# Causal convolution and RWKV channel mix on one core: a convolution in 64x64 tiles of TensorE, and three scalings per step on GpSimd

## Chip, cores and metric

The kernel runs on one core of a Trainium2 chip. The metric is device time of the launch in microseconds (us); lower is better.

## What is computed

The input x is [8, 4160, 192]. A light-weight convolution comes first: each of 8 heads owns 24 channels and has 7 taps, softmax-normalised, and an output row is the weighted sum of its own row and the six before it. The result y goes into an RWKV channel mix with d_ff = 1024:

```
y[b,s,h,:]  = sum_k softmax(weight[h])[k] * x_pad[b, s+k, h, :]      (6 zero rows ahead)
y_prev      = y one row earlier (zero at the start)
xk          = mu_k*y + (1-mu_k)*y_prev
xr          = mu_r*y + (1-mu_r)*y_prev
k           = relu(xk @ w_k)
v           = (k*k) @ w_v
out         = sigmoid(xr @ w_r) * v
```

The kernel works in bf16 with fp32 accumulation and writes fp32.

## The kernel before

**Pairs and steps.** The eight batches form four pairs. Both batches of a pair (`s` in the code's tiles) are worked on together: their channels stand side by side, 64 of the one in partitions 0-63 and 64 of the other in 64-127, three thirds (`NC`) of 64 channels each. A pair is cut into steps of 512 rows (256 at both ends of the first pair; the 64 rows left over of all four pairs make one last step), 34 steps in all, numbered 0 to 33.

**Bundles.** The order of all instructions is written out by hand. The unit is the bundle: four slots of the K product (`k_mm`, L458: 64-row tiles of TensorE, one for each batch of the pair), then the R product (`r`, L532) of an earlier step, then a V product (`v`, L515: 32 matmuls of 128x128 weights and 192 columns), then one or two calls of the convolution (`conv`). A step of 512 rows has two bundles. Tables (`early`, `first`, `rq`, `xt`, `mixes`, `vq`, `vo`, `late`) say what runs in which bundle, and the loop at L701 to L722 walks through them: `early`, K and its relus on ScalarE (L487), R, V, `mixes`, three squares of k on VectorE (L501), `vo` (the product with r, L556, and the DMA of the output), `xt` (the convolution), the fourth square, `late`.

**Mixtures.** `diff` (L411) forms y - y_prev for a step in the bundle ahead of it, on VectorE; there, too, `mix(s, 0)` forms xk: three scalings by mu (L434, one for each third) and an add (L438). `mix(s, 1)` forms xr in the same way one bundle later (for steps of two bundles). All of it is VectorE's. xk and xr have two buffers, the differences three.

**PSUM.** One ring of four slots of two banks serves K, R, V and the convolution in the order of issue: per bundle four K slots, one R, one V and one for each call of the convolution. A slot comes free when its reader (relu, sigmoid, the product at L556, or the copies of the convolution) has ended.

**Convolution.** It runs in blocks of 120 output rows: 128 input rows (6 of halo, 2 unused) lie in partitions, and a banded 128x128 matrix per head, `toe`, is the stationary operand. Blocks are gathered in groups; the first pair has groups of 3, 4, 4 and 5 blocks, whose results go back to channel-major form by TensorE transposes (`tr`), and then of 10 and 9; the others have 10, 10, 10 and 5. The later groups ("large": `on_pe` is False, index g above 3) take the way through DRAM: ScalarE copies the result to `y` (`conv_out`, L324), SP writes it to `y_dram` (`y_write`, L337), and a transposing DMA reads it back to `yT` (`y_read`, L345). For a group of 10 blocks a head is one matmul of 480 columns (10 blocks x 2 batches x 24 channels, L285), which fills a bank; a call does two heads, with one ring slot. A head that crosses a boundary of 64 channels has two copies.

**Loads of x.** `x_tile` takes one of three `xb` buffers and clears what has to be zero; `load_x` issues the DMAs, which cast to bf16, on GpSimd's queue (POOL): one for each batch (L125), and a smaller one at the start (L119) and at the end (L124) of a sequence. `keep_tail` (L395) copies a pair's last rows on GpSimd. Nothing else runs on GpSimd in the steady state.

Of the kernel before, what the change touches and what calls it, by code (L numbers as in the profile page):

```python
# [7 lines left out]
FP32 = mybir.dt.float32  # L8
BF16 = mybir.dt.bfloat16
# [5 lines left out]
def kernel(  # L15
# [11 lines left out]
    nc = tc.nc  # L27
# [8 lines left out]
    NC = D // Q  # L36
    HALO = K - 1
    BLK = 120
    GB = 10
    NBLK = -(-S // BLK)  # L40
    BANK = 512
# [40 lines left out]
    last_bundle = [bundle_of[st[3] + st[4] - 1] for st in steps]  # L82


    groups = []
    for p in range(NPAIR):
        blk0 = 0
        for nb, s, on_pe in (
            ((3, 0, True), (4, 1, True), (4, 2, True), (5, 3, True), (10, 4, False), (9, 6, False))
            if p == 0  # L90
            else ((10, 0, False), (10, 2, False), (10, 4, False), (5, 7, False))
        ):
            groups.append((p, blk0, nb, first_bundle[first_step[p] + s], on_pe))
            blk0 += nb


# [2 lines left out]
    def x_tile(g):  # L99
        p, blk0, nb, _, _ = groups[g]  # L100
        xb = three.tile([P, GB, 2, D], BF16, tag="xb", name="xb")
        xbs[g] = xb
        if g > 4:

            nc.vector.memset(xb[0:1, 0, 0, 0:2], 0.0)  # L105
        if blk0 == 0:
            nc.gpsimd.memset(xb[0:32, 0, :, :], 0.0)
        if blk0 + nb == NBLK:
            nc.gpsimd.memset(xb[:, nb - 1, :, :], 0.0)

    def load_x(g):
        p, blk0, nb, _, _ = groups[g]
        xb = xbs[g]
        for s in range(2):
            b = 2 * p + s
            lo, hi = 0, nb
            if blk0 == 0:
                lo = 1
                nc.gpsimd.dma_start(out=xb[HALO:P, 0, s, :], in_=x[b, 0 : P - HALO, :])  # L119
            t0 = blk0 * BLK - HALO  # L120
            if blk0 + nb == NBLK:
                hi = nb - 1
                r0 = t0 + hi * BLK
                nc.gpsimd.dma_start(out=xb[0 : S - r0, hi, s, :], in_=x[b, r0:S, :])  # L124
            nc.gpsimd.dma_start(  # L125
                out=xb[:, lo:hi, s, :],
                in_=bass.AP(
                    tensor=x.tensor,
                    offset=x.offset + (b * S + t0 + lo * BLK) * D,
                    ap=[[D, P], [BLK * D, hi - lo], [1, D]],  # L130
                ),
            )
# [134 lines left out]
    ys, yTs, y_drams = {}, {}, {}  # L267
    conv_ps = {}

    def chunks(g):  # L270
        n = max(1, min(3, BANK // (2 * G * groups[g][2])))
        return [range(h, min(H, h + n)) for h in range(0, H, n)]


    def conv_mm(g, c):
        nb = groups[g][2]
        if c == 0:
            ys[g] = two.tile([P, GB, 2 * D], BF16, tag="y", name="y")
        ps2 = ring.tile([P, 2, BANK], FP32, tag="k", name="ps_c")
        for k, hs in enumerate(chunks(g)[c : c + 2]):  # L280
            w = G * len(hs)
            ps = ps2[:, k, 0 : nb * 2 * w].rearrange("p (n s c) -> p n s c", n=nb, s=2)
            conv_ps[g, c + k] = ps
            for i, h in enumerate(hs):
                nc.tensor.matmul(  # L285
                    out=ps[:, :, :, i * G : (i + 1) * G],
                    lhsT=toe[:, h, :],
                    rhs=xbs[g][:, :nb, :, h * G : (h + 1) * G],
                    start=True,
                    stop=True,  # L290
                )

    def conv_small(g, copies):

        nb = groups[g][2]
        ys[g] = [two.tile([P, 4, P], BF16, tag=f"y_small{i}", name="y_small") for i in range(NC)]
        tiles = [ring.tile([P, 2, BANK], FP32, tag="k", name="ps_c") for _ in range(3 if g == 0 else 2)]
        banks = [t[:, i, 0 : nb * P] for t, i in ((tiles[0], 0), (tiles[1], 0), (tiles[-1], 0 if g == 0 else 1))]
        for i, o in enumerate(banks):
            o = o.rearrange("p (n s c) -> p n s c", n=nb, s=2)  # L300
            c0, c1 = i * Q, (i + 1) * Q
            for h in range(c0 // G, -(-c1 // G)):
                a, b = max(c0, h * G), min(c1, h * G + G)
                nc.tensor.matmul(
                    out=o[:, :, :, a - c0 : b - c0],
                    lhsT=toe[:, h, :],
                    rhs=xbs[g][:, :nb, :, a:b],
                    start=True,
                    stop=True,
                )  # L310
        for i, o in enumerate(banks):
            copies[i](out=ys[g][i][:BLK, :nb, :].rearrange("p n c -> p (n c)"), in_=o[:BLK, :])

    def conv_out(g, c, copy):
        nb = groups[g][2]
        hs = chunks(g)[c]
        ps = conv_ps.pop((g, c))
        y = ys[g][:BLK, :nb, :].rearrange("p n (c s q) -> p n c s q", c=NC, s=2)
        c0, c1 = hs[0] * G, hs[-1] * G + G
        a = c0  # L320
        while a < c1:
            i = a // Q
            b = min(c1, (i + 1) * Q)
            copy(out=y[:, :, i, :, a - i * Q : b - i * Q], in_=ps[:BLK, :, :, a - c0 : b - c0])  # L324
            a = b

    def new_yT(p):
        yTs[p] = two.tile([P, 3, -(-(YC + NBLK * BLK) // 16) * 16], BF16, tag="yT", name="yT")
        y_drams[p] = dram.tile([NBLK * BLK, 2 * D], BF16, tag=f"y{p % 2}", name="y_dram")
        nc.vector.memset(yTs[p][:, :, 0:YC], 0.0)  # L330


    def y_write(g):
        p, blk0, nb, _, _ = groups[g]
        if blk0 == 0:
            new_yT(p)
        nc.sync.dma_start(  # L337
            out=y_drams[p][blk0 * BLK : (blk0 + nb) * BLK, :].rearrange("(n t) c -> t n c", t=BLK),
            in_=ys[g][:BLK, :nb, :],
        )  # L340

    def y_read(g):
        p, blk0, nb, _, _ = groups[g]
        r0, r1 = blk0 * BLK, min((blk0 + nb) * BLK, S)
        nc.sync.dma_start_transpose(  # L345
            out=yTs[p][:, :, YC + r0 : YC + r1], in_=y_drams[p][r0:r1, :]
        )
# [67 lines left out]
    def mix(s, i, sl=slice(0, NC)):  # L415

        L = steps[s][2]
        d = diffs[s]
        if sl.start == 0:
            (xks, xrs)[i][s] = two.tile([P, NC, STEP], BF16, tag=("xk", "xr")[i], name=("xk", "xr")[i])  # L420
        t = (xks, xrs)[i][s]
        if s == 0 and i == 0:
            c = sl.start
            nc.vector.scalar_tensor_tensor(
                out=t[:, c, :L],
                in0=d[:, c, :L],
                scalar=mu[:, i, c : c + 1],
                in1=y_of(s, sl, 0)[:, 0, :],
                op0=ALU.mult,
                op1=ALU.add,  # L430
            )
            return
        for c in range(sl.start, sl.stop):
            nc.vector.tensor_scalar(  # L434
                out=t[:, c, :L], in0=d[:, c, :L], scalar1=mu[:, i, c : c + 1], scalar2=None, op0=ALU.mult
            )
        o = shaped(s, t[:, sl, :L])
        nc.vector.tensor_tensor(out=o, in0=o, in1=y_of(s, sl, 0), op=ALU.add)  # L438
# [151 lines left out]
    def at(table, b, fn, *a):  # L590
        table.setdefault(b, []).append((fn, a))

    def conv(g, c):
        if g < 3:
            act_, dve_ = nc.scalar.copy, nc.vector.tensor_copy
            return conv_small(g, (act_, act_, dve_ if g == 0 else act_))
        conv_mm(g, c)
        for k in range(c, min(c + 2, len(chunks(g)))):
            conv_out(g, k, nc.scalar.copy)

    for g, (p, blk0, nb, fb, on_pe) in enumerate(groups):
        nx = 1 if g < 3 else -(-len(chunks(g)) // 2)
        if g == 0:
            continue
        if g == 1:
            xs = []
        elif p == 0:
            xs = {2: [0], 3: [1, 1], 4: [2, 2, 3, 3], 5: [4, 4, 5, 5]}[g]
        else:
            xs = range(fb - 10, fb - 10 + nx)  # L610
        for i, b in enumerate(xs):
            at(xt, b, conv, g, 2 * i)
        if on_pe:
            for j in range((nb + 3) // 4):
                at(first, g - 1, tr, g, j)
        else:
            at(late, xs[-1], y_write, g)

            at(late, xs[-1] + (1 if g == 4 else 2), y_read, g)
        if g > 3:  # L620

            b = {4: 1, 5: 1, 6: 2, 7: 8, 8: 10, 9: 13}.get(g)
            b = first_bundle[first_step[p]] + (-17, -13, -7, -4)[(g - 6) % 4] if b is None else b
            at(early, b, x_tile, g)
            at(early, b, load_x, g)
# [127 lines left out]
```

## Time and profile before

| | us |
|---|---|
| median of 13 runs | 436.01 (435.67 to 438.3) |
| profiled execution, whole | 436.23 |
| its span on the core | 434.4 |
| TensorE busy | 422.0 |
| VectorE busy | 380.1 |
| ScalarE busy | 349.1 |
| GpSimd busy | 48.6 |

One execution is profiled; its span is the time between the first and the last instruction on the core, and 1.8 us of the execution lie around it. L-numbers are lines of the kernel before. A timeline line gives the start, the duration from the first start to the last end, the engine, the line and the operation, the operands with their shapes, and how many instructions the line stands for; in brackets, how long the engine had been idle and what ended that. PE is TensorE, PEld its weight loads, DVE VectorE, ACT ScalarE, POOL GpSimd, SP SyncE. The ends of matmuls are modelled and overlap the next start, so lengths of stages on TensorE are taken from start to start. A line of the shares by stage holds the stretch, its length, the busy times (with the number of instructions) of PE, PEld, DVE, ACT and POOL, the granted clock of TensorE, the share of the DMA engines and GB/s.

### The profile page before, as it was taken

How to read it: one execution, taken by the hardware profiler on the slowest of the kernel's cores; microseconds unless marked ns; L12 is line 12 of the kernel's file. 1: busy time of each engine (PE TensorE's matmuls, PEld its weight loads, DVE VectorE, ACT ScalarE, POOL GpSimd, SP SyncE). 2: the span in 40 equal slices, each digit the busy share in tenths (PEclk: the TensorE clock that was granted, in tenths of full speed). 3: DMA queues.
4: the chain of work that ended last, by engine and by line, in shares of the span. 5: the costliest groups of instructions: out<-in, count | busy, mean ns of one | idle time of the engine just before them, and what ended most of it. 6: DMA issues, size and time to landing. Idle time of an engine off the chain costs nothing.

```text
span 434.4 us, 11361 instructions
## 1 busy us (share of the span) xinstructions
PE 422.0 (97%) x4709; PEld 294.7 (68%) x4709; DVE 380.1 (87%) x678; ACT 349.1 (80%) x474; POOL 48.6 (11%) x73
## 2 busy tenths in 40 slices
PE   8789999999999999999999999999999999999995
PEld 3465757766866776676677667766766776667785
DVE  6879879998988989889888998898898898999983
ACT  5788987988888788889888788988898788777780
POOL 7450001202300100202110100102000000000000
PEclk9999999999999999999999999999999999999999
DMA  8998666999797953879697982696744463421223
GB/s 133 192 154 141 177 172 130 210 199 178 174 175 206 176 163 93 129 184 184 172 177 164 186 171 79 136 229 127 179 118 129 123 159 117 114 66 47 74 74 110
DMA packets 134484, 64.30 MB, mean 148 GB/s; under 512 B 85132, under 2 KB 134048, under 8 KB 134432
## 3 DMA queue, kind: packets, MB, share of 16 engines
q1 hardware_dynamic: 96050, 48.31, 44.2%
q0 software_dynamic: 37488, 14.66, 29.1%
q8 instruction: 37, 0.61, 0.6%
q10 hardware_dynamic: 894, 0.61, 0.5%
q14 instruction: 15, 0.12, 0.1%
HBM read 29.92 MB, written 36.99 MB: 154 GB/s over the span
## 4 chain that ended last, share of the span: by engine, by line
PE 87%; DMA 5%; DVE 4%; ACT 1%; issue 1%; POOL 1%; SPq 0%; ACTq 0%
PE ps_v L515 39%; PE ps_k L458 36%; PE ps_r L532 7%; PE ps_c L285 4%; DMA wk<-in_moe_w_k_dram 2%; DMA y_dram<-y 2%; DMA yT<-y_dram 2%; DVE k L501 2%; ACT k_sb L487 1%; ACT y L324 1%; DVE yT L367 0%; DVE d L411 0%; DVE xk L434 0%; POOL xb L125 0%; PE ps_t L358 0%
## 5 line engine op out<-in xcount | busy, mean ns | idle before, releaser
L487 ACT ACTIVATE k_sb<-ps_k 128x1024 bf16<-128x1024 f32 x260 | 246.6, 1053 | 25.8 <-PE ps_k L458 25.3
L515 PE MATMUL ps_v<-wv,k 128*128 128x192 bf16 x2080 | 182.7, 246 | 1.3 <-ACT k_sb L487 1.3
L458 PE MATMUL ps_k<-xk,wk 64*128 64x512 bf16 (+1 forms) x1632 | 181.1, 367 | 2.4 <-DVE xk L438 1.0
L515 PEld LDWEIGHTS <-k 128*128 128x128 bf16 x2080 | 168.7, 98 | 11.3 <-issue 11.3
L501 DVE TENSOR_TENSOR k<-k_sb 128x1024 bf16<-128x1024 bf16 x260 | 167.8, 686 | 0.4 <-ACT k_sb L487 0.4
L458 PEld LDWEIGHTS <-wk 64*128 64x128 bf16 x1632 | 74.7, 94 | 97.6 <-issue 19.1
L556 DVE TENSOR_TENSOR o_sb<-ps_v,r_sb 128x768 f32<-128x768 f32 x64 | 61.2, 956 | 35.2 <-PE ps_v L515 33.3
L324 ACT CAST y<-ps_c 120x480 bf16<-120x480 f32 (+4 forms) x134 | 54.3, 483 | 44.1 <-PE ps_c L285 44.1
L540 ACT ACTIVATE r_sb<-ps_r 128x768 bf16<-128x768 f32 x65 | 56.4, 867 | 1.3 <-PE ps_r L532 1.3
L125 POOL DMA_DIRECT2D xb<-in_x_dram x34 | 30.8, 911 | 210.9 <-PE ps_k L458 165.0
L532 PEld LDWEIGHTS <-xr 64*128 64x128 bf16 x780 | 34.1, 94 | 16.8 <-issue 1.4
L532 PE MATMUL ps_r<-wr,xr 64*128 64x192 bf16 x780 | 42.9, 243 | 1.6 <-DVE xb L105 0.8
L434 DVE TENSOR_SCALAR xk<-d,mu 128x512 bf16<-128x512 bf16 (+1 forms) x99 | 33.0, 388 | 1.2
L411 DVE TENSOR_TENSOR d<-yT 128x1536 bf16<-128x1536 bf16 (+2 forms) x35 | 31.0, 887 | 1.9 <-DMA yT<-y_dram 1.8
L438 DVE TENSOR_TENSOR xr<-xr,yT 128x1536 bf16<-128x1536 bf16 (+1 forms) x33 | 31.0, 939 | 1.1
L438 DVE TENSOR_TENSOR xk<-xk,yT 128x1536 bf16<-128x1536 bf16 (+1 forms) x32 | 30.4, 950 | 1.1
L434 DVE TENSOR_SCALAR xr<-d,mu 128x512 bf16<-128x512 bf16 (+1 forms) x102 | 29.0, 339 | 0.0
L285 PE MATMUL ps_c<-xb,toe 128*128 128x480 bf16 (+2 forms) x120 | 28.7, 338 | 0.0
L285 PEld LDWEIGHTS <-toe 128*128 128x128 bf16 x120 | 11.0, 98 | 1.0
L395 POOL COPY y_tail<-yT 128x195 bf16<-128x195 bf16 x4 | 1.9, 484 | 78.4 <-DMA yT<-y_dram 78.4
L651 PE MATMUL warm<-zeros,ones_t 128*128 128x512 bf16 x16 | 6.3, 578 | 1.8 <-DVE zeros L666 1.8
L367 DVE COPY yT<-ps_t 128x720 bf16<-128x720 bf16 (+1 forms) x7 | 3.2, 500 | 4.1 <-PE ps_t L358 4.1
(52 smaller groups left out, 51.2 us busy)
## 6 DMA issues: line engine op xcount, KB each, us to landing
out_dram<-o_sb SPq DMA_DIRECT2D x128, 192.0 KB, 2.4
y_dram<-y SPq DMA_DIRECT2D x10, 900.0 KB, 6.4
xb<-in_x_dram POOLq DMA_DIRECT2D x14, 480.0 KB, 8.7
xb<-in_x_dram POOLq DMA_DIRECT2D x6, 432.0 KB, 6.4
xb<-in_x_dram POOLq DMA_DIRECT2D x10, 192.0 KB, 6.3
y_dram<-y SPq DMA_DIRECT2D x3, 450.0 KB, 3.9
y_dram<-y SPq DMA_DIRECT2D x1, 810.0 KB, 5.7
xb<-in_x_dram POOLq DMA_DIRECT2D x2, 384.0 KB, 7.3
```

Of the source, the lines that this page charges most:

```text
L285: nc.tensor.matmul(out=ps[:, :, :, i * G : (i + 1) * G], lhsT=toe[:, h, :], rhs=xbs[g][:, :nb, :, h * G : (h + 1) * G], start=True, stop=True,
L324: copy(out=y[:, :, i, :, a - i * Q : b - i * Q], in_=ps[:BLK, :, :, a - c0 : b - c0])
L411: nc.vector.tensor_tensor(out=shaped(s, diffs[s][:, cs, :L]), in0=y_of(s, cs, 1), in1=y_of(s, cs, 0), op=ALU.subtract)
L434: nc.vector.tensor_scalar(out=t[:, c, :L], in0=d[:, c, :L], scalar1=mu[:, i, c : c + 1], scalar2=None, op0=ALU.mult)
L438: nc.vector.tensor_tensor(out=o, in0=o, in1=y_of(s, sl, 0), op=ALU.add)
L458: nc.tensor.matmul(out=ps[:, i, f * L : (f + 1) * L], lhsT=wk[r, c, fs], rhs=xk[r, c, :L], start=c == 0 and f == 0, stop=c == NC - 1 and f ...
L487: nc.scalar.activation(out=k_sb, in_=ps.rearrange("p a b -> p (a b)"), func=AF.Relu)
L501: nc.vector.tensor_tensor(out=o, in0=i, in1=i, op=ALU.mult)
L515: nc.tensor.matmul(out=o, lhsT=k2s[s][:, f, t * P : (t + 1) * P], rhs=wv[:, f, :], start=(f == 0), stop=(f == NF - 1),)
L532: nc.tensor.matmul(out=ps[:, i, k * D : (k + 1) * D], lhsT=xr[q, c, ts], rhs=wr[q, c, :], start=c == 0, stop=c == NC - 1,)
L540: nc.scalar.activation(out=r_sbs[s, j], in_=ps[:, :, 0 : 2 * D], func=AF.Sigmoid)
L556: nc.vector.tensor_tensor(out=o_sb.rearrange("p (b t) d -> p b (t d)", b=2), in0=v_ps.pop((s, j)), in1=r_sbs.pop((s, j)), op=ALU.mult,)
```

## The change

For the large groups a block of 116 rows takes the place of one of 120. It holds two half blocks of 58 output rows. The first one's 64 input rows lie in partitions 0-63, the second one's in 64-127. Each head is then four matmuls with 64x64 weights (the two diagonal quarters of `toe`): input half i goes to bank i, and the first and the second half of the group's blocks (j) go to output partitions 0-63 and 64-127. For a group of 10 blocks a matmul has 240 columns, and a unit of two heads fills both banks of a slot; ScalarE copies both banks in one instruction (two where a boundary of 64 channels is crossed). The end groups have 10 blocks in the first pair and 6 in the others, and the latter stand one step earlier in the order. The loads have a DMA for each batch and half, and further ones for rows at either end of a sequence. The write to `y_dram` is four DMAs: for each half of the partitions, 48 rows and 10. The read begins and ends at multiples of 16 rows. The fourth group (g = 3) keeps 128x128 matmuls in a function of its own, with its copies after both banks' matmuls. From step 3 on, the three scalings of xr run on GpSimd; its add stays on VectorE.

```
-            ((3, 0, True), (4, 1, True), (4, 2, True), (5, 3, True), (10, 4, False), (9, 6, False))
+            ((3, 0, True), (4, 1, True), (4, 2, True), (5, 3, True), (10, 4, False), (10, 6, False))
             if p == 0
-            else ((10, 0, False), (10, 2, False), (10, 4, False), (5, 7, False))
+            else ((10, 0, False), (10, 2, False), (10, 4, False), (6, 6, False))
...
+    def load_x_halves(g):
+        p, _, nb, _, _ = groups[g]
+        xb = xbs[g]
+        for s in range(2):
+            b = 2 * p + s
+            for i in range(2):
+                full = []
+                for m in range(nb):
+                    r0 = base[g] + (2 * m + i) * HB - HALO
+                    lo, hi = max(0, -r0), min(Q, S - r0)
+                    if lo == 0 and hi == Q:
+                        full.append(m)
+                    elif hi > lo:
+                        nc.gpsimd.dma_start(
+                            out=xb[i * Q + lo : i * Q + hi, m, s, :], in_=x[b, r0 + lo : r0 + hi, :]
+                        )
+                nc.gpsimd.dma_start(
+                    out=xb[i * Q : (i + 1) * Q, full[0] : full[-1] + 1, s, :],
...
+    def conv_units(g):
+        n = min(H, BANK // (G * groups[g][2]))
         return [range(h, min(H, h + n)) for h in range(0, H, n)]
...
+        for k, h in enumerate(hs):
+            for j in range(2):
+                for i in range(2):
+                    nc.tensor.matmul(
+                        out=ps[j * Q : (j + 1) * Q, i, 0 : nb * w].rearrange("p (n s c) -> p n s c", n=nn, s=2)[
+                            :, :, :, k * G : (k + 1) * G
+                        ],
+                        lhsT=toe[i * Q : (i + 1) * Q, h, i * Q : (i + 1) * Q],
+                        rhs=xbs[g][i * Q : (i + 1) * Q, j * nn : (j + 1) * nn, :, h * G : (h + 1) * G],
+                        start=True,
+                        stop=True,
+                    )
...
     def conv_out(g, c, copy):
...
+        src = ps[:, :, 0 : nb * (c1 - c0)].rearrange("p i (n s c) -> p i n s c", n=nb // 2, s=2)
+        y = ys[g][:, :nb, :].rearrange("p (n i) (c s q) -> p i n c s q", i=2, c=NC, s=2)
+        for a, b in pieces(c0, c1):
+            copy(out=y[:, :, :, a // Q, :, a % Q : a % Q + b - a], in_=src[:, :, :, :, a - c0 : b - c0])
...
     def y_write(g):
...
+        for j in range(2):
+            r0 = base[g] + j * nb * HB
+            rows = y_drams[p][r0 : r0 + nb * HB, :].rearrange("(n t) c -> t n c", t=HB)
+            for t0, t1 in ((0, HB // 16 * 16), (HB // 16 * 16, HB)):
+                nc.sync.dma_start(out=rows[t0:t1], in_=ys[g][j * Q + t0 : j * Q + t1, :nb, :])
...
     def y_read(g):
...
-        r0, r1 = blk0 * BLK, min((blk0 + nb) * BLK, S)
+        r0 = base[g] // 16 * 16
+        r1 = min((base[g] + 2 * nb * HB) // 16 * 16, S)
...
+        eng = nc.gpsimd if i == 1 and s > 2 else nc.vector
         for c in range(sl.start, sl.stop):
-            nc.vector.tensor_scalar(
+            eng.tensor_scalar(
                 out=t[:, c, :L], in0=d[:, c, :L], scalar1=mu[:, i, c : c + 1], scalar2=None, op0=ALU.mult
             )
```

More of the change, by code (lines that the diff above doesn't have):

```diff
@@ L38 @@
     BLK = 120
+    HB = 58
     GB = 10
@@ L82 @@
     last_bundle = [bundle_of[st[3] + st[4] - 1] for st in steps]
-    groups = []
+    groups, base = [], []
     for p in range(NPAIR):
@@ L88 @@
         for nb, s, on_pe in (
-            ((3, 0, True), (4, 1, True), (4, 2, True), (5, 3, True), (10, 4, False), (9, 6, False))
+            ((3, 0, True), (4, 1, True), (4, 2, True), (5, 3, True), (10, 4, False), (10, 6, False))
             if p == 0
-            else ((10, 0, False), (10, 2, False), (10, 4, False), (5, 7, False))
+            else ((10, 0, False), (10, 2, False), (10, 4, False), (6, 6, False))
         ):
             groups.append((p, blk0, nb, first_bundle[first_step[p] + s], on_pe))
+            if on_pe:
+                base.append(blk0 * BLK)
+            elif groups[-2][4] or blk0 == 0:
+                base.append(blk0 * BLK)
+            else:
+                base.append(base[-1] + 2 * HB * groups[-2][2])
             blk0 += nb
@@ L107, in x_tile @@
             nc.gpsimd.memset(xb[0:32, 0, :, :], 0.0)
-        if blk0 + nb == NBLK:
+        if g > 3 and base[g] + 2 * HB * nb >= S:
             nc.gpsimd.memset(xb[:, nb - 1, :, :], 0.0)
+    def load_x_halves(g):
[16 more added lines that the diff above has]
+                    out=xb[i * Q : (i + 1) * Q, full[0] : full[-1] + 1, s, :],
+                    in_=bass.AP(
+                        tensor=x.tensor,
+                        offset=x.offset + (b * S + base[g] + (2 * full[0] + i) * HB - HALO) * D,
+                        ap=[[D, Q], [2 * HB * D, len(full)], [1, D]],
+                    ),
+                )
     def load_x(g):
         p, blk0, nb, _, _ = groups[g]
+        if g > 3:
+            return load_x_halves(g)
         xb = xbs[g]
@@ L120, in load_x @@
             t0 = blk0 * BLK - HALO
[L121 to L124, printed above, removed]
             nc.gpsimd.dma_start(
@@ L268, with pieces @@
     conv_ps = {}
-    def chunks(g):
-        n = max(1, min(3, BANK // (2 * G * groups[g][2])))
+    def pieces(c0, c1):
+        cuts = [c0] + [a for a in range(Q, D, Q) if c0 < a < c1] + [c1]
+        return list(zip(cuts, cuts[1:]))
+    def conv_units(g):
+        n = min(H, BANK // (G * groups[g][2]))
         return [range(h, min(H, h + n)) for h in range(0, H, n)]
@@ L278, in conv_mm, with conv_full @@
             ys[g] = two.tile([P, GB, 2 * D], BF16, tag="y", name="y")
-        ps2 = ring.tile([P, 2, BANK], FP32, tag="k", name="ps_c")
[L280 to L284, printed above, removed]
+        ps = ring.tile([P, 2, BANK], FP32, tag="k", name="ps_c")
+        hs = conv_units(g)[c]
+        w = G * len(hs)
+        nn = nb // 2
+        conv_ps[g, c] = ps
+        for k, h in enumerate(hs):
[9 more added lines that the diff above has]
+                        stop=True,
+                    )
+    def conv_full(g, c, copy):
+        nb = groups[g][2]
+        if c == 0:
+            ys[g] = two.tile([P, GB, 2 * D], BF16, tag="y", name="y")
+        y = ys[g][:BLK, :nb, :].rearrange("p n (c s q) -> p n c s q", c=NC, s=2)
+        ps2 = ring.tile([P, 2, BANK], FP32, tag="k", name="ps_c")
+        w = 2 * G
+        banks = [ps2[:, k, 0 : nb * 2 * w].rearrange("p (n s c) -> p n s c", n=nb, s=2) for k in range(2)]
+        for k, ps in enumerate(banks):
+            for i in range(2):
+                h = 4 * c + 2 * k + i
                 nc.tensor.matmul(
@@ L290, in conv_mm @@
                     stop=True,
+                )
+        for k, ps in enumerate(banks):
+            c0 = (4 * c + 2 * k) * G
+            for a, b in pieces(c0, c0 + w):
+                copy(
+                    out=y[:, :, a // Q, :, a % Q : a % Q + b - a], in_=ps[:BLK, :, :, a - c0 : b - c0]
                 )
@@ L315, in conv_out @@
         nb = groups[g][2]
-        hs = chunks(g)[c]
+        hs = conv_units(g)[c]
         ps = conv_ps.pop((g, c))
-        y = ys[g][:BLK, :nb, :].rearrange("p n (c s q) -> p n c s q", c=NC, s=2)
         c0, c1 = hs[0] * G, hs[-1] * G + G
[L320 to L325, printed above, removed]
+        src = ps[:, :, 0 : nb * (c1 - c0)].rearrange("p i (n s c) -> p i n s c", n=nb // 2, s=2)
+        y = ys[g][:, :nb, :].rearrange("p (n i) (c s q) -> p i n c s q", i=2, c=NC, s=2)
+        for a, b in pieces(c0, c1):
+            copy(out=y[:, :, :, a // Q, :, a % Q : a % Q + b - a], in_=src[:, :, :, :, a - c0 : b - c0])
     def new_yT(p):
         yTs[p] = two.tile([P, 3, -(-(YC + NBLK * BLK) // 16) * 16], BF16, tag="yT", name="yT")
-        y_drams[p] = dram.tile([NBLK * BLK, 2 * D], BF16, tag=f"y{p % 2}", name="y_dram")
+        y_drams[p] = dram.tile([S + 2 * P, 2 * D], BF16, tag=f"y{p % 2}", name="y_dram")
         nc.vector.memset(yTs[p][:, :, 0:YC], 0.0)
@@ L336, in y_write @@
             new_yT(p)
[L337 to L340, printed above, removed]
+        for j in range(2):
[3 more added lines that the diff above has]
+                nc.sync.dma_start(out=rows[t0:t1], in_=ys[g][j * Q + t0 : j * Q + t1, :nb, :])
     def y_read(g):
         p, blk0, nb, _, _ = groups[g]
-        r0, r1 = blk0 * BLK, min((blk0 + nb) * BLK, S)
+        r0 = base[g] // 16 * 16
+        r1 = min((base[g] + 2 * nb * HB) // 16 * 16, S)
         nc.sync.dma_start_transpose(
@@ L596, in conv @@
             return conv_small(g, (act_, act_, dve_ if g == 0 else act_))
+        if g == 3:
+            return conv_full(g, c, nc.scalar.copy)
         conv_mm(g, c)
-        for k in range(c, min(c + 2, len(chunks(g)))):
-            conv_out(g, k, nc.scalar.copy)
+        conv_out(g, c, nc.scalar.copy)
     for g, (p, blk0, nb, fb, on_pe) in enumerate(groups):
-        nx = 1 if g < 3 else -(-len(chunks(g)) // 2)
+        nx = len(conv_units(g))
         if g == 0:
@@ L611 @@
         for i, b in enumerate(xs):
-            at(xt, b, conv, g, 2 * i)
+            at(xt, b, conv, g, i)
         if on_pe:
```

## The prediction

> **What bounds the kernel.** The page's busy shares come first, then the shares by stage, then the timeline of one period.
>
> ```profile
> PE 422.0 (97%) x4709; PEld 294.7 (68%) x4709; DVE 380.1 (87%) x678; ACT 349.1 (80%) x474; POOL 48.6 (11%) x73
> ...
> 160.00:200.00 40.00, 40.00 (x449) 28.04 (x444) 35.85 (x63) 34.54 (x48) 5.28 (x8) 1.00 0.62 134
> ```
>
> From 80 us on TensorE never stops. Starts, not modelled ends, give the bundle's length: one with a convolution, then one without.
>
> ```profile
> 201.32 2.76 PE L458 MATMUL ps_k<-xk,wk 64*128 64x512 bf16 x24
> 203.92 0.66 PE L532 MATMUL ps_r<-wr,xr 64*128 64x192 bf16 x12
> 204.51 2.81 PE L515 MATMUL ps_v<-wv,k 128*128 128x192 bf16 x32
> 207.16 0.57 PE L285 MATMUL ps_c<-xb,toe 128*128 128x480 bf16 x2
> 207.66 2.77 PE L458 MATMUL ps_k<-xk,wk 64*128 64x512 bf16 x24
> ...
> 379.37 2.81 PE L515 MATMUL ps_v<-wv,k 128*128 128x192 bf16 x32
> 382.11 2.76 PE L458 MATMUL ps_k<-xk,wk 64*128 64x512 bf16 x24
> ```
>
> 6.34 us (207.66-201.32) against 5.94 (382.11 less 376.18, the K start before it). The convolution costs 0.50 before K, but V is followed after 2.65 instead of 2.74: 0.405 in all, 0.20 for 480 columns.
>
> VectorE is nearly full in every second bundle, that with `diff` (call it A):
>
> ```profile
> 202.50 0.95 DVE L411 TENSOR_TENSOR d<-yT 128x1536 bf16<-128x1536 bf16 x1
> 203.49 0.88 DVE L434 TENSOR_SCALAR xk<-d,mu 128x512 bf16<-128x512 bf16 x3
> 204.40 0.96 DVE L438 TENSOR_TENSOR xk<-xk,yT 128x1536 bf16<-128x1536 bf16 x1
> 205.28 1.89 DVE L501 TENSOR_TENSOR k<-k_sb 128x1024 bf16<-128x1024 bf16 x3
> 207.36 0.96 DVE L556 TENSOR_TENSOR o_sb<-ps_v,r_sb 128x768 f32<-128x768 f32 x1 [0.20 <-PE ps_v L515]
> ...
> 62.77 0.95 DVE L556 TENSOR_TENSOR o_sb<-ps_v,r_sb 128x768 f32<-128x768 f32 x1
> 63.77 1.47 PE L458 MATMUL ps_k<-xk,wk 64*128 64x512 bf16 x12 [0.22 <-DVE o_sb L556]
> ```
>
> It waits 0.20 us in A before `o_sb`, and 0.88 in the other bundle (B). The last two lines show what lateness hits: K's second half (its 13th matmul) needs the PSUM slot that `o_sb` frees. In the steady state that half is due at 207.66+1.30 = 208.96 and `o_sb` ends at 208.32, so A tolerates 0.20+0.64, about 0.8 us of VectorE delay.
>
> **What the Trainium skill says.** "TensorEngine Tiling (Array Packing)", Key Properties: a change of tiling mode drains TensorE. The trace agrees: V to K takes 2.74, V to the convolution in the same 128x128 mode 2.65, so 0.095 for a switch. "SBUF — State Buffer", Who interferes with whom: GpSimd's port pair is VectorE's second, held by one instruction at a time; it collides with two-port modes, and a VectorE operation with two SBUF inputs collides with a GpSimd one that reads SBUF. The trace shows both a cost and none:
>
> ```profile
> 103.50 0.83 DVE L501 TENSOR_TENSOR k<-k_sb 128x1024 bf16<-128x1024 bf16 x1
> 104.18 0.37 POOL L395 COPY y_tail<-yT 128x195 bf16<-128x195 bf16 x1
> 104.26 0.83 DVE L501 TENSOR_TENSOR k<-k_sb 128x1024 bf16<-128x1024 bf16 x1
> ...
> 377.75 0.95 DVE L411 TENSOR_TENSOR d<-yT 128x1536 bf16<-128x1536 bf16 x1
> 378.10 0.82 POOL L395 COPY y_tail<-yT 128x195 bf16<-128x195 bf16 x1 [78.36 <-DMA yT<-y_dram]
> 378.75 0.88 DVE L434 TENSOR_SCALAR xk<-d,mu 128x512 bf16<-128x512 bf16 x3
> ```
>
> Around the first copy two squares take 0.83 instead of 0.68, 0.30 together; so at the two copies near 199 and 299 us (three squares 2.19 instead of 1.89). At the fourth the copy waits, and VectorE loses nothing. "DMA: Bandwidth & Descriptors", how many engines: the outermost sizes decide it, 16 for 48 rows, 10 for 10; this trace doesn't show it.
>
> **The change, part by part.**
>
> *Convolution on TensorE.* Two matmuls of 480 become, per bundle, two heads of four 64x64 matmuls of 240. Bounds of a four: 0.10 if all run together (half of 0.20), 0.20 if only the row halves do. The closest spacing in the trace of a load and a matmul is R's, (0.59-0.095)/12 = 0.041, so four take 0.10 to 0.16 by that; I take 0.13. A bundle: 2x0.13, plus one more mode switch, 0.095, is 0.355: 0.05 saved on the path, in 11x4 = 44 bundles 2.2 us. The three end groups spend 2x0.405 each now; then three units (3, 3 and 2 heads), 8x0.13+3x0.095 = 1.33, so they lose 1.6. Sum: 0.6 us saved. Ends: 5 us saved (0.10: 44x0.11, end groups even), 10 if the switch costs nothing more, 6 lost (0.20: 44x0.095, plus 1.6).
>
> *ScalarE.* A group of ten has 6x0.570+2x0.447+2x0.311 = 4.9 us of copies (by-shape means). Two of 960 elements and two each of 640 and 320, at about 0.8 ns an element more, take 4.2. V waits for the second relu after these copies by little, so nothing is gained; at worst the single copy's later start costs V 0.1 in a bundle.
>
> *R's scalings.* 31 steps (3 to 33) move three instructions each, no DMA. VectorE loses 0.90 us of work in B, where it was idle for 0.88 already: no gain on the path. GpSimd starts them when `diff` ends, in A (xr's buffer has been read two bundles before). They follow x's memsets and DMA issues on POOL's queue, which wait for convolutions at least two bundles old; `y_tail`'s copy and later loads queue behind them, with 5 us or more to spare. GpSimd itself: its memset of 384 took 0.42 and of one element 0.10, 0.82 ns an element, so 512 with COPY's fixed 0.2 take about 0.62; three, 1.9, of the 5.4 us from `diff`'s end to R's add (203.45 to 208.84, where its scalings start now). With a six-issue load ahead the add may wait 1 us, a few times, inside B's idle time.
> What it takes from VectorE: COPY took 0.30 for 195 elements; 317 more at 0.82 ns give 0.56; a scaling of VectorE that it meets leaves the port idle for about 0.16 of its 0.29 pitch (0.345 against 0.279 for 256 elements, so 0.13 goes with the 512). I take 0.40 each; ends 0 (the copy at 378.10) and 0.79 (COPY's cost by elements). Three delay A by 1.2. Behind that stand xk's scalings, its add, the squares and `o_sb`. Late by 1.2, less the 0.80, and K's second half is due 0.05 earlier: a stall of 0.45. Without a convolution the fourth K tile is the one due, 382.11+1.95 = 384.06, against an `o_sb` that starts at 382.43: 0.68 to spare, stall 0.52. A bundles with a convolution: 23; without: 8. 23x0.45+8x0.52 = 14.5 us.
>
> *DRAM round trip.* Four issues on SP instead of one, about 0.4 us each (0.45 at most steady issues), ahead of out's writes; later reads come two bundles behind. Only the first large group is bare: its write (7.56 us) and read (7.35) are on the chain at 43 to 58 us, where VectorE waits 1.8 for them. I charge 0.5; ends -0.5 and 1.5.
>
> *x loads.* Four to six POOL issues for two to four, about 0.75 for half a transfer against 0.95; landing within 10 us, and the users come 30 us later. Nothing; without that cover a microsecond a group. The earlier slot of the end group and the fourth group's reordered copies: nothing.
>
> Sum: -0.6+14.5+0.5 = 14.4. The profiled execution took 436.23 (span 434.4, 1.8 around it), close to the median 436.01. I forecast **450 us**.
>
> **Rivals.** (1) *The port hardly matters*: GpSimd fits into VectorE's gaps, as at 378.10, and the fours run together. Decided by three scalings costing under 0.8 us: no stall, and 5 us saved, 431; with a free switch 426. For it: the clean slack in B, the fourth copy. Against: three of four copies cost. (2) *A wash*: the delay lies just at the 0.8 tolerance and a four takes 0.13-0.16: 435.5 to 437. (3) *The fours are serial*, 0.20, and the port costs 0.40: 6+14.5+0.5, 457; decided by weight loads that don't overlap. (4) *Full lock*, 0.56: A late by 1.7, stalls 0.9 to 1.0, 23x0.93+8x1.0 = 29: 465; at 0.79 beyond 480.
>
> **Numbers.** Forecast (437 to 455) 0.45; rival 1 0.27; rival 2 0.08; rival 3 0.10; rival 4 0.10. 0.2% is what a measurement of this kernel can tell from no change. Faster 0.28, same 0.07, slower 0.65. The range, 428 to 460, leaves out rival 4 and the best of rival 1. Both signs hold chance, but the likeliest case alone has 437 to 455.
>
> **What would show it.** Each step right: in A bundles VectorE's time from `diff` to `o_sb` grows by about 1.2 us and K's 13th matmul waits for `o_sb`; V-to-K with a convolution falls from 3.15 to 3.10. Wrong: TensorE's starts stay gapless and bundles are 6.24 or shorter (rival 1), or the convolution takes 0.5 and more (rival 3), or R's matmuls wait for GpSimd.

## Result and profile after

The changed kernel takes 467.81 us (median of 10 runs, 466.19 to 471.76) against 436.22 for the kernel before (46 runs): a ratio of 1.0728, interval 1.0712 to 1.0744. It is 31.6 us slower; the forecast was 450, with a range up to 460. The profiled execution's span is 466.4 us. From here on an L-number is a line of the kernel whose profile is shown.

First the page of the changed kernel: busy shares, TensorE's busy tenths and its granted clock in 40 slices. After them two stretches from the shares by stage, one with an end group's load and one without.

```profile
PE 429.8 (92%) x5045; PEld 301.1 (65%) x5045; DVE 374.1 (80%) x585; ACT 348.4 (75%) x427; POOL 232.0 (50%) x194
...
PE   7789999696999999996899999999599999999996
...
PEclk9999999999799999999799999999799999999999
```

```profile
200.00:240.00 40.00, 34.20 (x386) 23.92 (x384) 28.31 (x45) 26.90 (x33) 17.18 (x19) 0.91 0.64 139
...
360.00:400.00 40.00, 40.00 (x487) 28.14 (x482) 35.93 (x54) 33.12 (x40) 18.77 (x10) 1.00 0.57 142
```

VectorE is less busy than before (374 us in a longer span), so it has not become full. TensorE's row has three notches at nearly equal distances (the 6, 6 and 5 in slices 10, 19 and 29), each with a notch in the clock in the same slice or the next; an earlier one, in slice 8, has none. Between 360 and 400 us TensorE is busy throughout. So most of the loss is made in a few places. One of them, in order of time (`diff`, after which the scalings could start; VectorE's memset of one element; GpSimd's load issues and scalings; then what waits):

```profile
204.29 0.95 DVE L473 TENSOR_TENSOR d<-yT 128x1536 bf16<-128x1536 bf16 x1
...
210.37 0.06 DVE L112 MEMSET xb<- 1x1 uint32 x1
...
211.65 0.69 POOL L134 DMA_DIRECT2D xb<-in_x_dram  x1 [11.19 <-issue]
...
214.77 0.71 POOL L134 DMA_DIRECT2D xb<-in_x_dram  x1
...
215.51 4.65 POOL L497 TENSOR_SCALAR xr<-d,mu 128x512 bf16<-128x512 bf16 x3
...
220.19 1.08 DVE L501 TENSOR_TENSOR xr<-xr,yT 128x1536 bf16<-128x1536 bf16 x1 [9.76 <-POOL xr L497]
...
221.96 3.77 ACT L550 ACTIVATE k_sb<-ps_k 128x1024 bf16<-128x1024 f32 x4 [5.71 <-DVE k L564]
...
223.04 1.47 PE L521 MATMUL ps_k<-xk,wk 64*128 64x512 bf16 x6 [5.80 <-ACT k_sb L550]
...
225.40 4.18 PE L578 MATMUL ps_v<-wv,k 128*128 128x192 bf16 x32
```

GpSimd sat idle for 11.2 us: the end group's load stands ahead of the bundle's scalings on its queue, and did not start before VectorE had reached the memset that `x_tile` puts into the same bundle (1.2 us after it; the profile names no releaser here, but does in an experiment below). After six issues and three scalings R's add starts; VectorE has stood idle for 9.76 us. The squares stand behind the add in VectorE's order, the relus wait for the squares' buffers, and K waits for the relus' PSUM slots: 5.80 us without a matmul. Afterwards the clock is low (the trace has 0.50 granted between 222 and 228 us): V's 32 matmuls take 4.18 us instead of 2.81. From 223.04 to the next convolution at 229.50 there are 6.46 us for work that takes 4.0 at the usual spacing, so this place costs about 8.3. Waits of these three kinds in the changed kernel, added up (total, times, longest):

```profile
DVE xr L501 <- POOL xr L497: 45.3, 11, 9.8
...
PE ps_k L521 <- ACT k_sb L550: 16.9, 4, 5.8
...
PE ps_k L521 <- DVE o_sb L619: 5.6, 10, 1.7
```

The bundle that the prediction worked with, A, in the changed kernel. Compare `diff`, xk's scalings (0.88 before), the squares (1.89 before), `o_sb` and K:

```profile
347.37 0.95 DVE L473 TENSOR_TENSOR d<-yT 128x1536 bf16<-128x1536 bf16 x1
...
348.36 1.31 DVE L497 TENSOR_SCALAR xk<-d,mu 128x512 bf16<-128x512 bf16 x3
...
348.52 5.80 POOL L497 TENSOR_SCALAR xr<-d,mu 128x512 bf16<-128x512 bf16 x3 [6.86 <-DVE d L473]
...
350.59 2.30 DVE L564 TENSOR_TENSOR k<-k_sb 128x1024 bf16<-128x1024 bf16 x3
...
352.39 2.89 PE L521 MATMUL ps_k<-xk,wk 64*128 64x512 bf16 x24
352.51 1.02 ACT L385 CAST y<-ps_c 128x320 bf16<-128x320 f32 x2 [0.93 <-PE ps_c L321]
352.81 0.94 DVE L619 TENSOR_TENSOR o_sb<-ps_v,r_sb 128x768 f32<-128x768 f32 x1
```

VectorE loses 0.43 and 0.41, some 0.85 us in all, while three scalings run for 5.8 us beside it. The trace shows that just two of its instructions lose the time: the second of xk's scalings takes 0.78 us and its neighbours 0.35 and 0.34, and the second of the three squares takes 1.10 instead of 0.68. GpSimd loses too: its second scaling takes 2.50 us, the others 1.63 and 1.72. K is stretched by 0.13 only (2.89 for 2.76). The convolution, V to K:

```profile
245.56 2.81 PE L578 MATMUL ps_v<-wv,k 128*128 128x192 bf16 x32
...
248.30 0.40 PE L321 MATMUL ps_c<-xb,toe 64*64 64x240 bf16 x8
248.63 1.47 PE L521 MATMUL ps_k<-xk,wk 64*128 64x512 bf16 x12
```

3.07 us instead of 3.15.

### The profile page after: what moved, and what is told of

The parts are those of the page before. It is cut to its first block, busy times and chain, and to the rows that moved or that the text cites. A ratio compares the mean times of both kernels' runs of the same rounds, so it can differ in the third digit from the quotient of the medians.

```text
span 466.4 us, 12099 instructions
## 1 busy us (share of the span) xinstructions
PE 429.8 (92%) x5045; PEld 301.1 (65%) x5045; DVE 374.1 (80%) x585; ACT 348.4 (75%) x427; POOL 232.0 (50%) x194
## 5 line engine op out<-in xcount | busy, mean ns | idle before, releaser
L497 POOL TENSOR_SCALAR xr<-d,mu 128x512 bf16<-128x512 bf16 (+1 forms) x93 | 169.4, 1833 | 125.8 <-DVE d L473 84.2
L521 PE MATMUL ps_k<-xk,wk 64*128 64x512 bf16 (+1 forms) x1632 | 187.3, 370 | 25.7 <-ACT k_sb L550 16.9
L578 PE MATMUL ps_v<-wv,k 128*128 128x192 bf16 x2080 | 186.2, 249 | 1.3 <-ACT k_sb L550 1.3
L564 DVE TENSOR_TENSOR k<-k_sb 128x1024 bf16<-128x1024 bf16 x260 | 178.6, 726 | 1.6 <-ACT k_sb L550 1.4
L578 PEld LDWEIGHTS <-k 128*128 128x128 bf16 x2080 | 171.8, 99 | 12.1 <-issue 11.8
L385 ACT CAST y<-ps_c 128x960 bf16<-128x960 f32 (+7 forms) x81 | 50.7, 667 | 60.4 <-PE ps_c L321 60.4
L619 DVE TENSOR_TENSOR o_sb<-ps_v,r_sb 128x768 f32<-128x768 f32 x64 | 60.8, 950 | 26.8 <-PE ps_v L578 24.8
L134 POOL DMA_DIRECT2D xb<-in_x_dram x56 | 40.9, 737 | 72.6 <-issue 39.5
L497 DVE TENSOR_SCALAR xk<-d,mu 128x512 bf16<-128x512 bf16 (+1 forms) x99 | 39.6, 454 | 1.2
L321 PE MATMUL ps_c<-xb,toe 64*64 64x240 bf16 (+1 forms) x448 | 20.0, 265 | 0.0
L321 PEld LDWEIGHTS <-toe 64*64 64x64 bf16 x448 | 8.3, 105 | 7.7 <-issue 7.7
L131 POOL DMA_DIRECT2D xb<-in_x_dram x14 | 7.8, 556 | 2.9 <-DMA wr<-in_moe_w_r_dram 2.0
```

The lines of the kernel that those rows point to most:

```text
L134: nc.gpsimd.dma_start(out=xb[i * Q : (i + 1) * Q, full[0] : full[-1] + 1, s, :], in_=bass.AP(tensor=x.tensor, offset=x.offset + (b * S + b ...
L385: copy(out=y[:, :, :, a // Q, :, a % Q : a % Q + b - a], in_=src[:, :, :, :, a - c0 : b - c0])
L497: eng.tensor_scalar(out=t[:, c, :L], in0=d[:, c, :L], scalar1=mu[:, i, c : c + 1], scalar2=None, op0=ALU.mult)
L521: nc.tensor.matmul(out=ps[:, i, f * L : (f + 1) * L], lhsT=wk[r, c, fs], rhs=xk[r, c, :L], start=c == 0 and f == 0, stop=c == NC - 1 and f ...
L564: nc.vector.tensor_tensor(out=o, in0=i, in1=i, op=ALU.mult)
L578: nc.tensor.matmul(out=o, lhsT=k2s[s][:, f, t * P : (t + 1) * P], rhs=wv[:, f, :], start=(f == 0), stop=(f == NF - 1),)
```

## Experiments

Three theories stood after the profile. The **queue theory**: R's add waits for GpSimd, above all behind the end groups' loads. The **port theory**, that of the prediction: VectorE, held up by GpSimd after `diff`, makes `o_sb` late in every second bundle. The **data-path theory**: the way through DRAM has become slower.

### The convolution alone

```
-        eng = nc.gpsimd if i == 1 and s > 2 else nc.vector
+        eng = nc.vector
```

> The changed kernel with all of R's scalings back on VectorE: the convolution, its loads and its writes stay as changed. Queue theory (the loss is R's add waiting for GpSimd, above all behind the end groups' loads) and port theory (the loss is VectorE held up by GpSimd's port use after diff, so that o_sb comes late): both 431 to 434, as in the changed kernel V to K with a convolution takes 3.07 instead of 3.15, 53 x 0.08 = 4 saved. Data-path theory (the loss is in the round trip through DRAM with four writes and twice the loads): 450 or more.

Measured: 433.68 us, ratio 0.9932 (0.9905 to 0.9958). The convolution with its loads and writes saves 2.5 us (436.15 for the kernel before, run beside it), and the data-path theory falls. After 80 us the timeline shows a single wait of TensorE, 0.56 us. This is the fastest version of the study.

### The scalings alone

```
+        eng = nc.gpsimd if i == 1 and s > 2 else nc.vector
         for c in range(sl.start, sl.stop):
-            nc.vector.tensor_scalar(
+            eng.tensor_scalar(
```

(in the kernel before)

> The kernel before with only R's three scalings moved to GpSimd from step 3 on. Queue theory: R's add waits beside the loads again, a little less than in the changed kernel since the end groups have four POOL issues of about 2.7 us instead of six of 4.1: three places with 6 to 8 us of TensorE idle or slow, 455 to 466. Port theory: stalls of about 1 us in every second bundle, 458 to 468, spread evenly. Data-path theory: 436 to 442.

Measured: 467.28 us, ratio 1.0701 (1.0676 to 1.0726). So the scalings do nearly all of the damage, with either convolution. The total lies 1.3 us above what the queue theory expected (455 to 466) and inside the range of the port theory (458 to 468), so it doesn't decide. The place does: TensorE's three longest waits, 4.24 to 4.40 us, are at the end groups' loads, and between 360 and 440 us it has none. There the load looks like this:

```profile
210.44 0.06 DVE L105 MEMSET xb<- 1x1 uint32 x1
210.82 0.81 POOL L125 DMA_DIRECT2D xb<-in_x_dram  x1 [11.29 <-DVE xb L105]
...
212.96 4.64 POOL L435 TENSOR_SCALAR xr<-d,mu 128x512 bf16<-128x512 bf16 x3
...
217.63 1.08 DVE L439 TENSOR_TENSOR xr<-xr,yT 128x1536 bf16<-128x1536 bf16 x1 [7.13 <-POOL xr L435]
```

Here the releaser of the load is named outright: the memset on VectorE. The wait at R's add is 2.6 us shorter than in the changed kernel; here the scalings stand behind three issues after the memset, not six.

### The end groups' loads behind the scalings

```
-            at(early, b, x_tile, g)
-            at(early, b, load_x, g)
+            tail = g > 6 and (g - 6) % 4 == 3
+            at(late if tail else early, b, x_tile, g)
+            at(late if tail else early, b, load_x, g)
```

> The changed kernel; the three end groups' buffer clearing and loads are issued at the end of their bundle instead of its start, so that the scalings of that bundle are ahead of them on POOL's queue. Queue theory: the three waits of 9.8 us at R's add shrink to 3 or less (the next step's scalings now stand behind that load), TensorE keeps its clock there: about 3 x 6 = 18 less, 447 to 453. Port theory: within 3 us of the changed kernel, 465 to 468.

Measured: 454.51 us, ratio 1.0428 (1.0376 to 1.0481): 13.3 less, where 15 to 21 were expected. The port theory's 465 to 468 is excluded. The longest wait at R's add falls from 9.8 to 5.3 us, not to 3: the next step's scalings now stand behind this load.

### All loads behind the scalings, buffers cleared ahead

```
-            at(early, b, x_tile, g)
-            at(early, b, load_x, g)
+            if g < 7:
+                at(early, b, x_tile, g)
+                at(early, b, load_x, g)
+            else:
+                tail = (g - 6) % 4 == 3
+                at(early, b - 1 if tail else b, x_tile, g)
+                at(late, b if tail else b + 1, load_x, g)
```

> The changed kernel; from the second pair's second group on, the buffer is cleared one bundle ahead and the load issued after the scalings of the bundle, so that no scaling stands behind a load that waits or has yet to be issued. Queue theory: R's add waits under 5 us in all, no TensorE gap over 2 us after 130 us, 434 to 441; what is left above the version without GpSimd is VectorE's 0.85 us of delay in every second bundle. Port theory: 460 or more, since the scalings still meet VectorE right after diff.

Measured: 438.24 us, ratio 1.0041 (1.0030 to 1.0053), as the queue theory expected. The waits at R's add in this version:

```profile
DVE xr L501 <- POOL xr L497: 2.5, 3, 1.7
```

A different order on GpSimd's queue, with the same scalings on the same engine, thus takes away 467.81 - 438.24 = 29.6 us. The other 4.6 us, against the 433.68 of the convolution alone, remain although TensorE has no wait over 0.72 us after 60 us. K's starts near the end, first in this version, then in the one without GpSimd's scalings (in neither is there a convolution in these bundles):

```profile
385.12 2.91 PE L521 MATMUL ps_k<-xk,wk 64*128 64x512 bf16 x24
...
391.20 2.76 PE L521 MATMUL ps_k<-xk,wk 64*128 64x512 bf16 x24
...
397.13 2.91 PE L521 MATMUL ps_k<-xk,wk 64*128 64x512 bf16 x24
```

```profile
380.11 2.76 PE L521 MATMUL ps_k<-xk,wk 64*128 64x512 bf16 x24
...
386.05 2.76 PE L521 MATMUL ps_k<-xk,wk 64*128 64x512 bf16 x24
...
391.98 2.76 PE L521 MATMUL ps_k<-xk,wk 64*128 64x512 bf16 x24
```

A step takes 12.01 us (397.13-385.12) against 11.87, and the stretched K (2.91) is that behind bundle A: 0.14 a step, and with 29 steps of 512 rows 4.1 us. That is the effect that the port theory describes, VectorE late after `diff`, at its real size. That VectorE and GpSimd contend at the port, and not elsewhere, no run here shows; the traces show that they slow each other while they overlap.

### Only the clearing earlier

```
-            at(early, b, x_tile, g)
+            at(early, b - 1 if g > 6 and (g - 6) % 4 == 3 else b, x_tile, g)
```

> The changed kernel; only the clearing of the end groups' buffers (VectorE's one-element memset and GpSimd's memset) is issued one bundle earlier, and their loads stay ahead of the scalings on POOL's queue. Clearing theory (the long wait comes from a load that cannot start before VectorE has reached the memset in the same bundle): the loads run while GpSimd is idle anyway, the three waits of 9.8 us go, 3 x 8 less: 441 to 447. Length theory (six issues and three scalings of 1.55 us are too long whatever they wait for): the waits shrink by the 1 to 2 us at most that the memset cost, 461 to 466.

Measured: 451.44 us, ratio 1.0358 (1.0311 to 1.0405). The loads keep their place ahead of the scalings, and 16.4 us are gone: a memset of 0.06 us on another engine's queue held that much. The load followed the memset:

```profile
198.38 0.95 DVE L473 TENSOR_TENSOR d<-yT 128x1536 bf16<-128x1536 bf16 x1
198.39 0.06 DVE L112 MEMSET xb<- 1x1 uint32 x1
...
199.68 0.81 POOL L134 DMA_DIRECT2D xb<-in_x_dram  x1 [5.13 <-issue]
```

It began again 1.2 us after the memset, now beside `diff` and not a bundle later. The gain is less than the expected 21 to 27, since the scalings still stand behind its six issues: R's add waits 11 times, 26.8 us in all, at most 3.4. The length theory's 461 to 466 is excluded.

### The clearing earlier for all groups

```
-            at(early, b, x_tile, g)
+            at(early, b - 1 if g > 6 else b, x_tile, g)
```

> The same for all groups from the second pair's second on: every clearing one bundle earlier, loads where the change has them. Clearing theory: the remaining waits beside the other groups' loads go too, as in the version with the loads after the scalings (438.2): 436 to 441. Length theory: above 455.

Measured: 446.02 us, ratio 1.0224 (1.0201 to 1.0247), 5 us above what was expected. The timeline shows why:

```profile
213.18 0.41 POOL L114 MEMSET xb<- 32x384 bf16 x1 [10.23 <-DVE xb L112]
213.57 4.64 POOL L497 TENSOR_SCALAR xr<-d,mu 128x512 bf16<-128x512 bf16 x3
```

The shift brought the clearing of a pair's first group into a bundle that has scalings behind it. GpSimd's own memset, which also waits for VectorE's, took over the part of the load, and R's add waited 5.16 us here: the same mistake at another place.

### Why a scaling takes so long

The prediction took 0.62 us for a scaling. It has 1.88 on average: 1.55 where VectorE stands still (4.65 for three), 1.94 beside it (5.82 for three). Two kernels, each run once, leave out the product with mu_r: the first copies the difference, the second multiplies it by 0.5.

```
+            if eng is nc.gpsimd:
+                eng.tensor_copy(out=t[:, c, :L], in_=d[:, c, :L])
+                continue
```

> The changed kernel with GpSimd copying the difference instead of scaling it (the product with mu_r is left out from step 3 on). If a scaling is slow because of its operation (arithmetic with a scalar of each partition), a copy of 512 takes about 0.62 us as its copy of 195 and its memset suggest, and the kernel comes to 445 to 460; if it is slow because VectorE holds the port, the copy takes 1.5 us or more beside VectorE, too, and the time stays at 464 to 468.

```
+            if eng is nc.gpsimd:
+                eng.tensor_scalar(out=t[:, c, :L], in0=d[:, c, :L], scalar1=0.5, scalar2=None, op0=ALU.mult)
+                continue
```

> The changed kernel with GpSimd scaling by a constant 0.5 instead of mu_r (that product is changed from step 3 on). If reading a scalar for each partition is what makes the scaling slow, it falls towards 0.62 us; if it is the arithmetic of the scaling itself, it stays at 1.55 us alone and 1.9 beside VectorE, and the time at 464 to 468.

Measured: 460.55 us with copies, 470.85 with a constant (one execution each). Their groups, busy time and mean ns of one; copies first:

```profile
L498 POOL COPY xr<-d 128x512 bf16<-128x512 bf16 x87 | 59.4, 724 | 168.3 <-DVE d L473 158.2 <-PE ps_k L524 10.0
```

```profile
L498 POOL TENSOR_SCALAR xr<-d 128x512 bf16<-128x512 bf16 x87 | 143.6, 1671 | 126.8 <-DVE d L473 86.2 <-PE ps_k L524 30.2 <-PE ps_r L598 10.3
```

The copy behaves as the small rows had promised: 1.72 us for three behind the end group's load, 0.57 each. The scaling by a constant takes 1.48 alone (4.43 for three) and 1.67 on average. So the operation makes the difference, a multiplication instead of a copy; neither VectorE's presence nor chiefly the scalar of each partition does. And with copies the kernel is still 24 us slower than before, just above the 445 to 460 expected. With the constant it is above the expected 464 to 468, but within the 466.19 to 471.76 of the changed kernel's own runs, so no difference is shown. With this order on the queue, shorter instructions alone gave back only some 7 us.

### Writing 58 partitions at once

```
-            for t0, t1 in ((0, HB // 16 * 16), (HB // 16 * 16, HB)):
+            for t0, t1 in ((0, HB),):
```

(in the version with the convolution alone)

> The version without GpSimd scalings (433.7), with each half of a group's y written to DRAM as one DMA of 58 partitions instead of two of 48 and 10. If the outermost size decides how many DMA engines share a transfer, 58 rows go to two of them: a write takes well over 15 us instead of about 6, and as the read is issued two bundles (12.5 us) later and SP waits there, out's writes and the next diff are late: 440 to 470. If the split is only a matter of issue time, two issues fewer on SP: 433 to 434.

Measured: 531.47 us, ratio 1.2176 (1.2104 to 1.2248), far above the expected range, on the side of the shared-engine theory. The first large group's write and the read that waits for it, on SP's queue, in the version with 48 and 10 and then in this one:

```profile
43.53 3.05 SPq L401 DMA_DIRECT2D y_dram<-y  x4
...
50.32 3.72 SPq L407 DMA_TRANSPOSE yT<-y_dram  x1
```

```profile
44.71 8.17 SPq L401 DMA_DIRECT2D y_dram<-y  x2
52.98 11.28 SPq L627 DMA_DIRECT2D out_dram<-o_sb  x2
66.31 3.59 SPq L407 DMA_TRANSPOSE yT<-y_dram  x1
```

From the write's issue to the read's it is 6.8 us with 48 and 10 and 21.6 with 58. The latter isn't the write alone: its two issues hold SP's queue for 8.17 us, and two issues of `out` behind them for another 11.28. In the waits of this version `o_sb` stands for 70.5 us behind `out`'s transfers, which are issued from the same queue. The share of the 16 DMA engines (the figure before the last one) tells how many were at work, first with 48 and 10, then with 58:

```profile
44.00:49.00 5.00, 4.74 (x70) 3.76 (x66) 4.15 (x8) 4.30 (x6) 0.00 (x0) 1.00 0.83 195
...
46.00:63.00 17.00, 16.24 (x208) 12.30 (x204) 9.46 (x15) 15.60 (x20) 0.00 (x0) 1.00 0.14 46
```

16 x 0.83 is 13.3 and 16 x 0.14 is 2.2, which agrees with the two engines that were expected; which ones they were the trace doesn't tell. Without the parts of 48 and 10 the new tile shape would cost far more than it saves.

## Why the prediction was wrong

**Convolution.** The mechanism was right and the gain undersized: 0.6 us were predicted, 2.5 measured. A four takes (0.33-0.095)/2 = 0.117 with the switch of 0.095, where 0.13 was taken; V to K came to 3.07, not 3.10. At 44 bundles that is 44 x 0.08 = 3.5. The end groups' three units lengthen V to K by 0.32, 0.32 and 0.26 us, against two calls of 0.405: they lose 0.3 in all, not 1.6. These figures would give 3.2 us; why 0.7 of it is missing isn't known.

**Order on GpSimd's queue.** This is the step that failed. The prediction said that the scalings follow loads "which wait for convolutions at least two bundles old", and that with a six-issue load ahead "the add may wait 1 us, a few times, inside B's idle time". The end groups' loads wait for something much younger: VectorE's memset in the same bundle. So scalings that could have begun at the end of `diff` (205.24) began at 215.51. The add waited 9.1 to 9.8 us at three places, and B's 0.88 us of idle time was no match. What stopped was not R's matmuls, as in the prediction's sign of being wrong, but K, through squares and relus. The trace of before had shown the pattern, harmless then, as nothing stood behind it:

```profile
196.55 0.79 POOL L125 DMA_DIRECT2D xb<-in_x_dram  x1 [12.87 <-DVE xb L105]
```

Size by experiment: 29.6 of the 34.1 us that the scalings cost, where the prediction had put nothing.

**Length of a scaling.** 0.62 was a price for moving data (memset, COPY); multiplying takes 1.48 to 1.94. Three fill 5.8 us, more than the 5.4 us from `diff`'s end to R's add, which left no room for a load ahead of them. The copies show what the expected length would have been worth: some 7 us, in one execution.

**Port.** The path was right, a late `o_sb` that stretches K, and the size off. Three scalings took 0.85 us from VectorE, not 1.2, close to the tolerance of 0.80; the stall is 0.14 a step, not 0.45 to 0.52: 4.6 us in all instead of 14.5. The tolerance without a convolution was misread: `o_sb` starts at 382.34, not 382.43, which leaves 0.77 instead of 0.68 and would have made the forecast 0.7 us lower.

```profile
382.34 0.95 DVE L556 TENSOR_TENSOR o_sb<-ps_v,r_sb 128x768 f32<-128x768 f32 x1
```

"SBUF — State Buffer", Who interferes with whom, says that in VectorE's two-port modes the second instruction waits for the first one's whole length. No run shows in which mode xk's scalings ran; if in such a mode, the trace doesn't agree: the scaling of VectorE that met GpSimd's first one (348.52 to 350.14) began at 348.63 and ended at 349.41; it lost 0.43 us and did not wait until 350.14. Here the measurement decides: the cost was a fraction of the overlap.

**ScalarE, loads, DRAM round trip.** The order of size held. A load issue takes 0.74 us (0.75 predicted). In the version with the convolution alone the four write issues take 0.50 each in the median and 3.05 us together at the first large group, yet its read starts no later (50.32 against 50.80 before): the charge of 0.5 wasn't needed.

**Rivals.** The number lies next to that of the fourth, 465, but not its mechanism: it had asked for stalls of 0.9 to 1.0 in each step. That the number came close is chance. None of the rivals was the one that happened; of the port alone, rival 2 had the size, a delay just at the tolerance.

## What to carry over

When work moves to an idle engine with an in-order queue, list what stands ahead of each instruction there, and for each of these what it waits for: an idle engine that idles in a wait is not free. Price an operation from rows with the same arithmetic, not from rows that only move data. A buffer's clearing belongs ahead of the bundle in which its load is issued, but not in front of work that others wait for, as the version with all clearings earlier showed.

## Not expected of the hardware

GpSimd multiplied 512 bf16 elements of each partition by a constant in 1.48 us and by a scalar of each partition in 1.55, undisturbed, and copied them in 0.57. Where its scalings met VectorE's work, two single VectorE instructions of a bundle lost about 0.42 us each, and one of the three scalings took 2.50 us. Writing 58 partitions to DRAM at once kept 2.2 of 16 DMA engines busy for 17 us where 48 and 10 had kept 13.3 busy, and the whole kernel went from 433.7 to 531.5. After 5.8 us without a matmul TensorE ran slower for the following 6 us (granted clock 0.50 between 222 and 228 us, 0.91 over the 40 us around it), which added some 2.5 us at that place.
